# Block-sorted attention with a gated layer on one core: the whole program written as one list, with the picks on ScalarE, the first balancing round alone, six value groups read in place and the first up layer split by units

## The chip, the cores and the metric

One core of one Trainium2 chip runs the kernel. The metric is the device time of one execution in microseconds: 238.96 us for the kernel before, the median of three runs from 238.65 to 239.04.

## The reference

Four batches of eight heads, 768 positions and 64 dimensions. For each head an 8x8 matrix `P` is balanced five times, then keys and values are mixed block by block with it, each query block attends to one mixed block of 96 keys, and the result, heads side by side, goes through a layer with the gate `h * cos(h)`.

```python
for _ in range(5):
    P = P - np.max(P, axis=-1, keepdims=True)
    P = np.exp(P)
    P = P / (np.sum(P, axis=-1, keepdims=True) + 1e-09)
    P = P / (np.sum(P, axis=-2, keepdims=True) + 1e-09)
k_sorted = np.einsum('bhij,bhjcd->bhicd', P, k_b)
v_sorted = np.einsum('bhij,bhjcd->bhicd', P, v_b)
...
scores = scale * np.matmul(q_b, k_sb.transpose(0, 1, 2, 4, 3))
...
h = x @ w_in          # 3072 x 512 by 512 x 2048
g = h * np.cos(h)
return g @ w_out      # 2048 x 512
```

## The kernel before, in words

The 3072 rows are cut into eight chunks `n` of 384 rows; a chunk is half a batch and has four **units** `u` of 96 rows (one query block, all heads). Each chunk goes through scores, softmax, the products with the values (`av`), the turning of their result into `xT`, the up layer (`h`, a cosine on ScalarE, the gate on VectorE) and the down layer (`o`). Later chunks overlap: while chunk `n` is in its up and down layers, the attention of chunk `n+1` is slipped in between.

**The start.** `make_identity` builds `ident` on GpSimd. The loads of queries, keys and values of batch 0 are issued by GpSimd ahead of it, the weights behind. The balancing runs on 32 partitions (L326 to L354): per round one exp on ScalarE (L327) and six instructions on VectorE (L301 to L306). In round 0 the reduction `maskp` (L329), which reads `ident`, stands on VectorE ahead of the round's own six. After round 4 the balanced matrices are in `sorted_by`. `pick` holds zeros and ones: GpSimd clears it (L213) and writes the ones by `affine_select` (L207), three for batches 1, 0, 1 at the start and two for batches 2 and 3 later. A `block` is eight small matmuls of `pick` with `sorted_by` (L360); `spread` (L365) multiplies it with `maskp` into `bd`, the matrix that mixes the blocks. Queries of chunk 0 are turned on TensorE (L315) and copied by ScalarE (L321); `keep_warm` matmuls (L238) on a tile of zeros fill TensorE's waits.

**Keys and values of batch 0.** Three key groups `kp` (L375, 16 matmuls each) and eight value groups `v0` (L662, eight matmuls each) give mixed keys and values; each is copied out of PSUM by ScalarE or VectorE (`k_place`, `v0e`). A value matmul has as its weights the values of one dimension `d` over 96 positions. In `kv`, as loaded, these lie 64 elements apart. GpSimd can copy them into `vperm`, where they lie side by side (L179, 16 dimensions per copy). Before, groups 0 to 3 read `kv` and groups 4 to 7 read `vperm`, after two copies. A matmul writes `w` neighbouring results of 64 columns, of which the first counts and the others are overwritten by the next matmuls: `w` is 3 for groups 0 to 3 and 2 for 4 to 7, less at a group's end.

**Scores to xT, chunk 0.** For each unit: scores on TensorE (L681), maximum and subtraction on VectorE (L698, L702), exp on ScalarE (`p_buf`, L467), transposes on TensorE (L713), their copy `pT` (ScalarE or VectorE), `av` (L514), the division on VectorE (L525, L527), transposes `xps` (L722) and their copy into `xT`. PSUM has three large buffers (`big`) and two small ones (`acc`); a group waits until the copy of its buffer's last owner is done. The four units come in the order 0, 1, 3, 2. The value groups stand between them on TensorE: 3, 1, scores 0, 4, 5, scores 1, 6, 7, scores 3, transposes 0, 2, scores 2, 0.

**First up layer.** `up_four` (L735) makes chunk 0's up layer in halves: two units wide (192 columns), eight matmuls per call; half 0 needs `xT` of units 0 and 1.

The instructions of each engine stand in program order, written out call by call (L782 to L1097), and no engine but TensorE's weight loads departs from it.

Of the kernel before, what the change touches and what calls it, by code (L numbers as in the profile page):

```python
# [14 lines left out]
AX = mybir.AxisListType  # L15


@with_exitstack
def kernel(
# [15 lines left out]
    nc = tc.nc  # L35
# [169 lines left out]
    def picked(t, z, b):  # L205

        nc.gpsimd.affine_select(  # L207
            out=t[:, :, z * PB:(z + 1) * PB], in_=t[:, :, z * PB:(z + 1) * PB],
            compare_op=ALU.not_equal, fill=1.0, base=-b * PB,
            pattern=[[1, nb], [-1, PB]], channel_multiplier=nb)  # L210

    def picks(t, batches):
        nc.gpsimd.memset(t[:], 0.0)  # L213
        for z, b in enumerate(batches):
            picked(t, z, b)
# [7 lines left out]
    picks(pick, (1, 0, 1))  # L223
# [18 lines left out]
    keep_warm(15, big.tile([128, 512], FP32, name="idle", tag="big"))  # L242
# [34 lines left out]
    E, Q = E_eps[:, :, :nb], Q_eps[:, :nb]  # L277
# [21 lines left out]
    def normalize(it, out):  # L299

        nc.vector.reduce_sum(sums[0][:], E_eps[:], axis=AX.X)  # L301
        nc.vector.reciprocal(over[0][:], sums[0][:])
        nc.vector.tensor_tensor(Q, E, by_row(over[0]), op=ALU.mult)
        nc.vector.reduce_sum(sums[1][:], Q_eps.rearrange("p i j -> p j i"), axis=AX.X)
        nc.vector.reciprocal(over[(1, 2, 1, 3, 1)[it]][:], sums[1][:])
        nc.vector.tensor_tensor(out, Q, by_column(over[(1, 2, 1, 3, 1)[it]]), op=ALU.mult)  # L306
# [3 lines left out]
    def q_twice(h2):  # L310
        ps = turns[h2] = acc.tile([128, 2, IC, QR, blk // QR], BF16, name="qps", tag="acc")
        for hp in range(2):
            for r in range(QR):
                for x in range(2):
                    nc.tensor.transpose(  # L315
                        ps[x * D:(x + 1) * D, hp, :, r],
                        q_rows[:, h2 * 2 + hp, r * D:(r + 1) * D], ident[:blk, :blk])

    def q_place(h2):
        dst = q_turned[0][:, :, :QW].rearrange("d e (i h c) -> d h e i c", h=H2, c=blk)  # L320
        A.copy(dst[:, h2], turns.pop(h2).rearrange("d e i r p -> d e i (r p)"))  # L321

    def idle(times):
        keep_warm(times, acc.tile([128, 512], FP32, name="idle", tag="acc"))

    for it in range(5):  # L326
        nc.scalar.activation(E, less[:], AF.Exp)  # L327
        if it == 0:
            nc.vector.reduce_sum(  # L329
                maskp.rearrange("p (b e x) -> p b x e", b=2, e=2),  # L330
                ident.rearrange("p (b x e j) -> p b x e j", b=2, e=2, j=nb), axis=AX.X)
            A.copy(
                order.rearrange("k (p r) -> k p r", r=QR),
                ident[:blk, :blk].rearrange("k (r p) -> k p r", r=QR))
            q_twice(0)
            q_twice(1)
            keep_warm(2, big.tile([128, 512], FP32, name="idle", tag="big"))
        if it >= 2:
            q_place(it - 2)
            if it < 4:  # L340
                idle((6, 2)[it - 2])
                q_twice(it)
            else:
                idle(4)
                q_place(3)
        normalize(it, (less if it < 4 else sorted_by)[:])
        if it == 1:
            nc.gpsimd.tensor_copy(held[:B * H], over[2][:, :1])
            for z in range(3):
                load_w_in(z)  # L350
        if it == 3:
            nc.gpsimd.tensor_copy(held[:B * H], over[3][:, :1])
            load_w_in(3)
            load_q(1)  # L354

    def block(picked, pool=acc, tag="acc"):

        ps = pool.tile([128, nb], FP32, name="bl", tag=tag)
        for j in range(nb):
            nc.tensor.matmul(  # L360
                ps[:], picked[:, j], sorted_by[:, :, j], start=(j == 0), stop=(j == nb - 1))
        return ps

    def spread(dst, ps):
        nc.vector.tensor_tensor(  # L365
            dst[:], maskp.to_broadcast([128, 2 * H, nb]),
            ps[:].unsqueeze(1).to_broadcast([128, 2 * H, nb]), op=ALU.mult)

    blocks = [block(pick[:, :, z * PB:(z + 2) * PB]) for z in range(2)]
    spread(bds[0], blocks[0])  # L370

    MH = H2 * IC

    def k_products(ps, t, c, rows, rhs, keys=kbuf):
        nc.tensor.matmul(  # L375
            ps[:, t], keys[rows, c * 2 * D:(c + 1) * 2 * D], rhs, start=True, stop=True)

    def k_sort_g(t0, eng, pool, tag):
        ps = pool.tile([128, 4, 4 * NB], FP32, name="ks", tag=tag)
        for t in range(4):  # L380
            k_products(ps, t, t0 + t, slice(0, 128), bds[1].rearrange("p x i -> p (x i)"),
                       pair)
        copy_on(
            eng, kT2[:, ::2, :, :, t0:t0 + 4].rearrange("p e b m t -> p b e m t"),
            ps.rearrange("p t (b e m) -> p b e m t", b=2, e=2))

    def k_swap(keys):
# [3 lines left out]
    def hold_keys():  # L391

        nc.gpsimd.tensor_copy(held[:], kT[1][:, 1, 0, :1])
# [14 lines left out]
    def v_cols(d, permuted):  # L408
        return vperm[:, d * blk:d * blk + 128] if permuted else vv[:, d]

    def v_sort_b(b, d0, nd, eng, pool, tag):
        ps = pool.tile([128, nd, 2 * NB], FP32, name="vs", tag=tag)
        rows, xs = slice(0, 64 + b * 64), slice(b * H, (b + 1) * H)
        for t in range(nd):
            nc.tensor.matmul(
                ps[:, t], v_cols(d0 + t, b == 1 or d0 + t >= D // 2)[rows],
                bdv[rows, xs].rearrange("p x i -> p (x i)"), start=True, stop=True)
        copy_on(
            eng, vS[0][:, b * 2 * NB:(b + 1) * 2 * NB, d0:d0 + nd],
            ps[:blk].rearrange("p t n -> p n t"))  # L420

    def v_sort_g(d0, nd, eng, pool, tag):
        ps = pool.tile([128, nd, 4 * NB], FP32, name="vs", tag=tag)
        for t in range(nd):
            nc.tensor.matmul(  # L425
                ps[:, t], v_cols(d0 + t, True), bds[1].rearrange("p x i -> p (x i)"),
                start=True, stop=True)
        copy_on(eng, vS[1][:, :, d0:d0 + nd], ps[:blk].rearrange("p t n -> p n t"))

    def v_at(g, b2, hp, h2, i):  # L430
        return (b2 * 2 + hp) * NB + h2 * nb + i


    LATE = 5
    s_t, pb, pT, xn_t = {}, {}, {}, {}
    xT = {}
    cnt = [0]

    def qk_part(n, u, part, pool, tag):
        w = len(part)  # L440
        sc = pool.tile([128, w, 512], FP32, name="sc", tag=tag)
        for h2 in range(H2):
            for e, hp in enumerate(part):
                scores(sc[:, e, h2 * 128:h2 * 128 + blk], n, u, h2, hp)
        scv = sc[:blk].rearrange("p e (h c) -> p (e h) c", c=128)[:, :, :blk]
        mx = small.tile([blk, w * H2], FP32, name="mx", tag="mx")
        nc.vector.reduce_max(mx[:], scv, axis=AX.X)  # L447
        s = s_t[n, u][:, part[0]:part[0] + w].rearrange("p e h c -> p (e h) c")
        nc.vector.tensor_tensor(s, scv, mx.to_broadcast(list(s.shape)), op=ALU.subtract)  # L449

    def qk(n, u):

        s_t[n, u] = sp.tile([blk, 2, H2, blk], FP32, name="s", tag="s")
        qk_part(n, u, [0, 1], big, "big")

    def qk_half(n, u, hp, pool=None, tag="acc"):

        if hp == 0:
            s_t[n, u] = sp.tile([blk, 2, H2, blk], FP32, name="s", tag="s")
        qk_part(n, u, [hp], pool or acc, tag)  # L460

    def expo(n, u, on_pe=False):
        p = p_bufs[cnt[0] % NP]
        cnt[0] += 1


        nc.scalar.activation(  # L467
            p[:, :, :blk], s_t.pop((n, u)).rearrange("p e h c -> p (e h) c"), AF.Exp,
            scale=scale)
        if n < LATE:  # L470
# [6 lines left out]
        if on_pe:  # L477
            pb[n, u] = p
        else:
            nc.sync.dma_start_transpose(out=t[:], in_=p.rearrange("p a c -> p (a c)"))  # L480

    def hold(t):

        nc.gpsimd.tensor_copy(held[:blk], t[:blk, 0, :1])

    def p_hold(n, u):
        hold(pT[n, u])

    def p_transpose(n, u, eng, pool, tag):
        p = pb.pop((n, u))  # L490
        ps = pool.tile([128, 2 * H2, 128], BF16, name="pps", tag=tag)
        for a in range(2 * H2):
            nc.tensor.transpose(ps[:blk, a, :blk], p[:, a, :blk], ident[:blk, :blk])
# [646 lines left out]
```

## Time and profile before

| | |
|---|---|
| time, median of 3 | 238.96 us (238.65 to 239.04) |
| span of the profiled execution | 236.9 us |
| time minus span | 2.1 us (launch and end, outside the span; the profiled execution's own time is not listed apart from its span) |
| TensorE busy | 228.3 us (96%) |
| VectorE, ScalarE, GpSimd busy | 171.1, 154.0, 93.4 us |
| first matmul of chunk 0's up layer | 29.97 us |
| first matmul of chunk 0's down layer | 41.86 us |

Busy times of engines overlap. A busy TensorE may still be slow, since a matmul that waits for its weights counts as busy; so the time from the start of one matmul to the start of the next is what has to be read. Times in the timeline count from the span's start. A row such as `x8` merges eight neighbouring instructions, its second number is from the first one's start to the last one's end. "PEld" is the weight load of a matmul.

### The profile page before, as it was taken

Reading aid. Unit: us, or ns where it says so; the run is one execution under the profiler, and the core shown is the slowest. Engines: PE = TensorE matmul, PEld = TensorE weight load, DVE = VectorE, ACT = ScalarE, POOL = GpSimd, SP = SyncE. Lnnn points to the kernel's source line nnn. Section 1 sums busy time; section 2 is a strip of 40 time slices with the busy share of each in tenths; the row PEclk is TensorE's granted clock in tenths of the full one; section 3 lists DMA queues with packets and bytes.
Section 4 is the critical chain, followed back from the end, with each engine's and each line's share of the span. In section 5 each row is a group of like instructions: output and inputs, shape, how many; then the busy total and the mean of one; then the engine's idle time right before and its main releaser. Section 6 shows DMA issues by size and latency. Waiting matters only on the chain.

```text
span 236.9 us, 5429 instructions
## 1 busy us (share of the span) xinstructions
PE 228.3 (96%) x2230; PEld 144.0 (61%) x2230; DVE 171.1 (72%) x284; ACT 154.0 (65%) x205; POOL 93.4 (39%) x117
## 2 busy tenths in 40 slices
PE   8699999999999999999999999999999999999994
PEld 2368799567665656655666556655564565555553
DVE  5658976887789666893689976998698769535700
ACT  3356975588889747795688747673767376646611
POOL 7699994894970098940808000800000000000000
PEclk9999999999999999999999999999999999999999
DMA  7999999995899989869899938944972460341012
GB/s 97 203 199 205 203 224 211 148 201 167 102 117 183 146 155 136 160 150 184 95 104 101 116 64 150 209 68 91 119 216 46 80 192 3 55 133 47 0 44 89
DMA packets 66423, 30.89 MB, mean 130 GB/s; under 512 B 55136, under 2 KB 61920, under 8 KB 66144
## 3 DMA queue, kind: packets, MB, share of 16 engines
q0 software_dynamic: 24048, 13.64, 42.1%
q1 hardware_dynamic: 42064, 16.73, 33.4%
q8 instruction: 17, 0.28, 0.5%
q10 hardware_dynamic: 288, 0.20, 0.3%
q14 instruction: 6, 0.05, 0.1%
HBM read 27.27 MB, written 6.29 MB: 142 GB/s over the span
## 4 chain that ended last, share of the span: by engine, by line
PE 81%; DMA 6%; ACT 4%; DVE 4%; issue 3%; POOL 1%; SPq 0%; ACTq 0%; POOLq 0%
PE h L558 31%; PE o L583 21%; DMA pT<-p_buf 5%; PE h L735 5%; PE o L756 4%; PE sc L405 3%; PE av L514 3%; PE ks L375 2%; PE vs L662 2%; ACT p_buf L467 2%; PE o L1104 1%; PE vs L425 1%; PE pps L713 1%; DMA xT<-xn 1%; PE vs L238 1%
## 5 line engine op out<-in xcount | busy, mean ns | idle before, releaser
L558 PE MATMUL h<-xT,w_in_t 128*128 128x384 bf16 x448 | 78.4, 326 | 0.2 <-DMA xT<-xn 0.2
L583 PE MATMUL o<-w_out_t,gg 128*128 128x512 bf16 x320 | 76.5, 379 | 0.0
L566 DVE TENSOR_TENSOR gg<-c,h 128x768 bf16<-128x768 f32 x56 | 52.6, 949 | 18.8 <-ACT c L562 18.8
L562 ACT ACTIVATE c<-h,half_pi 128x768 f32<-128x768 f32 x56 | 50.4, 900 | 22.5 <-PE h L558 21.6
L558 PEld LDWEIGHTS <-w_in_t 128*128 128x128 bf16 x448 | 42.2, 98 | 26.5 <-issue 0.6
L583 PEld LDWEIGHTS <-gg 128*128 128x128 bf16 x320 | 29.1, 98 | 27.6
L467 ACT ACTIVATE p_buf<-s 96x768 bf16<-96x768 f32 x32 | 26.0, 840 | 4.4 <-DVE s L702 2.4
L179 POOL COPY vperm<-kv 64x1536 bf16<-64x1536 bf16 (+1 forms) x10 | 28.0, 2831 | 0.6 <-DMA kv<-in_v_dram 0.6
L449 DVE TENSOR_TENSOR s<-sc,mx 96x384 f32<-96x384 f32 (+1 forms) x33 | 24.3, 735 | 1.8
L447 DVE TENSOR_REDUCE mx<-sc 96x4 f32<-96x384 f32 (+1 forms) x33 | 24.0, 729 | 0.7 <-PE sc L405 0.7
L527 DVE TENSOR_TENSOR xn<-av,r 96x512 bf16<-96x512 f32 x32 | 22.0, 687 | 1.1
L525 DVE RECIPROCAL r<-av 96x8 f32<-96x8 f32 x32 | 6.4, 199 | 14.6 <-PE av L514 14.4
L129 POOL DMA_DIRECT2D kv<-in_q_dram x24 | 15.9, 674 | 0.7 <-issue 0.5
L405 PE MATMUL sc<-kTs,q_turned 128*128 128x96 bf16 x224 | 15.3, 206 | 0.1
L249 ACT COPY kv<-o 128x512 f32<-128x512 f32 (+2 forms) x10 | 5.3, 530 | 14.9 <-PE o L583 12.4
L405 PEld LDWEIGHTS <-q_turned 128*128 128x128 bf16 x224 | 12.6, 98 | 4.0 <-DVE s L449 0.4
L249 ACT CAST kTs<-ks 128x512 bf16<-128x512 f32 (+1 forms) x18 | 11.0, 632 | 5.7 <-PE ks L375 5.7
L756 PE MATMUL o<-w_out_t,gg 128*128 128x512 bf16 x48 | 11.4, 379 | 0.0
L251 DVE COPY kv<-o 128x512 f32<-128x512 f32 (+1 forms) x5 | 3.0, 602 | 11.4 <-PE o L1104 8.5
L129 POOL DMA_DIRECT2D q_mem<-in_q_dram x16 | 10.7, 684 | 1.2 <-DMA kv<-in_v_dram 1.0
L238 PE MATMUL idle<-warm 128*128 128x512 bf16 x29 | 8.5, 436 | 2.8 <-ACT q_turned L321 1.8
L735 PE MATMUL h<-xT,w_in_t 128*128 128x192 bf16 x128 | 11.1, 246 | 0.0
(119 smaller groups left out, 285.0 us busy)
## 6 DMA issues: line engine op xcount, KB each, us to landing
out_dram<-kv SPq DMA_DIRECT2D x12, 256.0 KB, 2.5
out_dram<-o_s SPq DMA_DIRECT2D x10, 256.0 KB, 2.7
w_in_t<-in_moe_w_in_dram POOLq DMA_DIRECT2D x4, 512.0 KB, 11.8
w_out_t<-in_moe_w_out_dram POOLq DMA_DIRECT2D x4, 512.0 KB, 12.6
kv<-in_k_dram POOLq DMA_DIRECT2D x2, 768.0 KB, 10.3
kv<-in_v_dram POOLq DMA_DIRECT2D x2, 768.0 KB, 13.1
pair<-in_k_dram POOLq DMA_DIRECT2D x2, 768.0 KB, 11.0
kv<-in_v_dram POOLq DMA_DIRECT2D x6, 256.0 KB, 5.4
```

The costliest lines, as they stand in the source:

```text
L129: nc.gpsimd.dma_start(out=q_heads[:, i, :, e], in_=src[:, ih * IC + i, :, e])
L179: nc.gpsimd.tensor_copy(dst, src)
L405: nc.tensor.matmul(out, q_of(n, hp)[:, x:x + 128], keys_of(n, u, h2, hp), start=True, stop=True)
L447: nc.vector.reduce_max(mx[:], scv, axis=AX.X)
L449: nc.vector.tensor_tensor(s, scv, mx.to_broadcast(list(s.shape)), op=ALU.subtract)
L467: nc.scalar.activation(p[:, :, :blk], s_t.pop((n, u)).rearrange("p e h c -> p (e h) c"), AF.Exp, scale=scale)
L527: nc.vector.tensor_tensor(xn.rearrange("p h e d -> p e h d"), avv[:, :, :, :D], r.to_broadcast([blk, 2, H2, D]), op=ALU.mult)
L558: nc.tensor.matmul(h[:, f2, :w], w_in_t[:, kk, f * 128:(f + 1) * 128], xT[n][:, kk], start=(kk == 0), stop=(kk == KC - 1))
L562: nc.scalar.activation(c[:], h[:, :, :w], AF.Sin, bias=half_pi[:, 0:1])
L566: nc.vector.tensor_tensor(gt[n, fp // 2][:, f:f + 2], c[:], h[:, :, :w], op=ALU.mult)
L583: nc.tensor.matmul(o[:], gt[n, f // 4][:, f % 4, ts * 128:(ts + 1) * 128], w_out_t[:, f, :], start=(f == 0), stop=(f == FC - 1))
L735: nc.tensor.matmul(o[:, part, f2 * w:(f2 + 1) * w], w_in_t[:, kk, f * 128:(f + 1) * 128], xT[0][:, kk, h * w:(h + 1) * w], start=(kk == 0) ...
```

## The change

All of L308 to L1097 becomes one text, `PLAN`, one call per line, which a loop reads; helpers are renamed and split so that each line issues work on one engine (`S` scores, `M` maximum, `X` subtraction, `E` exp, `TP`/`TE` transposes and their copy, `AV`/`N` products and division, `XP`/`XE` the turning into `xT`, `U`/`C`/`G` up, cosine, gate, `D`/`O`/`W` down, copy and store). What differs in the work:

- `maskp` and `order` (the other early copy) stand behind round 0 on VectorE and behind round 1's exp on ScalarE. First warm-up matmuls: 12 for 15, then 2, 6 and 4 for 2, 6, 2 and 4.
- The five `affine_select` are gone. `pick` is laid out with rows one element longer, so that its ones have a regular step, and ScalarE copies them from `ident`, three in the balancing, two between the last exp of chunk 0 and the copies `pT`.
- Value groups 0 to 5 read `kv` in place, only 6 and 7 read `vperm` (one copy of GpSimd, not two); every value matmul writes 64 columns, none of them overwritten. Order on TensorE: 0, 1, scores 0, 2, 3, 4, scores 1, 5, scores 2, transposes 0, 6, scores 3, 7. Units come in the order 0, 1, 2, 3. The fill matmuls ahead of the groups are seven as before.
- The first half of the first up layer runs by units: `U1` has 32 matmuls of 96 columns on `xT` of one unit, its cosine is one instruction, its gate two. Half 1 stays as it was.
- On GpSimd the values of batch 1 are loaded ahead of its keys, and the queries of chunk 2 behind the four `vperm` copies of batch 1.

From the first matmul of the down layer on, TensorE, VectorE, ScalarE and the store queue have the same instructions in the same order as before, but for the places named.

```diff
-    def picked(t, z, b):
-        nc.gpsimd.affine_select(
-            out=t[:, :, z * PB:(z + 1) * PB], in_=t[:, :, z * PB:(z + 1) * PB],
-            compare_op=ALU.not_equal, fill=1.0, base=-b * PB,
-            pattern=[[1, nb], [-1, PB]], channel_multiplier=nb)
+    def picked(first, n, z, b, eng):
+        w = n * PB + 1
+        d = pair[:B * H, first * PB * nb:first * PB * nb + nb * w].rearrange(
+            "p (j c) -> p j c", c=w)[:, :, z * PB:(z + 1) * PB].rearrange(
+            "p j (h i) -> p h j i", i=nb)[:, :, :, 0]
+        copy_on(eng, d, ident[:B * H, b * H:(b + 1) * H].unsqueeze(2).to_broadcast([B * H, H, nb]))
...
-    for it in range(5):
-        nc.scalar.activation(E, less[:], AF.Exp)
-        if it == 0:
-            nc.vector.reduce_sum(
-                maskp.rearrange("p (b e x) -> p b x e", b=2, e=2),
...
+    VZ, v_wide = 6, 1
...
-            w = min(8 - t, 2 if z > 3 else 3)
+            w = min(8 - t, v_wide)
             nc.tensor.matmul(
-                o[:, t:t + w].rearrange("p w n -> p (w n)"), v_cols(z * 8 + t, z > 3)[:64],
+                o[:, t:t + w].rearrange("p w n -> p (w n)"), v_cols(z * 8 + t, z >= VZ)[:64],
...
+    def U1(u, g):
+        o = kept_tile(("h1", u, g), big, "big", [128, 2, 512], FP32, "h")
+        for z in range(8):
+            f = g * 8 + z
+            for kk in range(KC):
+                nc.tensor.matmul(
+                    o[:, z // 4, z % 4 * blk:(z % 4 + 1) * blk],
+                    w_in_t[:, kk, f * 128:(f + 1) * 128],
+                    xT[0][:, kk, u * blk:(u + 1) * blk], start=(kk == 0), stop=(kk == KC - 1))
+    def G1(u, g, b):
+        if (0, g * 2 + b) not in gt:
+            gt[0, g * 2 + b] = gp.tile([128, 4, TC], BF16, name="gg", tag="gg")
+        nc.vector.tensor_tensor(
+            gt[0, g * 2 + b][:, :, u * blk:(u + 1) * blk],
+            ps["c1", u, g][:, b].rearrange("p (f c) -> p f c", f=4),
+            ps["h1", u, g][:, b, :TC].rearrange("p (f c) -> p f c", f=4), op=ALU.mult)
...
+    for line in PLAN.split("\n"):
+        name, *args = line.split()
```

On VectorE, the start of the first balancing round, before (`P` is the loaded matrix, `less` the input of the exp, `E` its output):

```order
L296 TENSOR_REDUCE top<-P 32x8
L297 TENSOR_TENSOR less<-P,top 32x64
L329 TENSOR_REDUCE maskp<-ident 128x2x4x2
L301 TENSOR_REDUCE sums_150<-E 32x8
L302 RECIPROCAL over_152<-sums_150 32x8
L303 TENSOR_TENSOR Q<-E,over_152 32x64
```

and now:

```order
L1147 TENSOR_TENSOR less<-P,top 32x64
L1151 TENSOR_REDUCE sums_137<-E 32x8
L1152 RECIPROCAL over_139<-sums_137 32x8
L1153 TENSOR_TENSOR Q<-E,over_139 32x64
L1154 TENSOR_REDUCE sums_138<-Q 32x8
L1155 RECIPROCAL over_140<-sums_138 32x8
L1156 TENSOR_TENSOR less<-Q,over_140 32x64
L1196 TENSOR_REDUCE maskp<-ident 128x2x4x2
```

`maskp`, and with it the wait for `ident`, moved from ahead of the round to behind it.

On ScalarE, from the copies of the value groups (`vS`) to the first cosine (`c`), before (`p_buf` is an exp of chunk 0, `pT` and `xT` are copies of transposes):

```order
L249 CAST vS<-vs 96x64x8 x3
L467 ACTIVATE p_buf_106<-s 96x8x96
L249 CAST vS<-vs 96x64x8 x2
L467 ACTIVATE p_buf_107<-s 96x8x96
L249 CAST vS<-vs 96x64x8
L249 COPY pT<-pps 96x768
L249 CAST vS<-vs 96x64x8
L467 ACTIVATE p_buf_108<-s 96x8x96
L467 ACTIVATE p_buf_106<-s 96x8x96
L249 COPY pT<-pps 96x768 x2
L249 COPY xT<-xps 128x4x96
L741 ACT_TABLE_LOAD
```

and now:

```order
L1388 ACTIVATE p_buf_106<-s 96x8x96
L1099 CAST vS<-vs 96x64x8
L1388 ACTIVATE p_buf_107<-s 96x8x96
L1099 CAST vS<-vs 96x64x8 x2
L1099 COPY pT<-pps 96x768
L1099 CAST vS<-vs 96x64x8
L1388 ACTIVATE p_buf_108<-s 96x8x96
L1388 ACTIVATE p_buf_106<-s 96x8x96
L1099 COPY pair<-ident 32x8x8 x2
L1099 COPY pT<-pps 96x768 x2
L1099 COPY xT<-xps 128x4x96
L1544 ACT_TABLE_LOAD
```

The second exp stands one value copy earlier, and two pick copies (`pair<-ident`) stand between the last exp and the last two `pT`.

On GpSimd, around the copies of batch 1's values into `vperm`, before:

```order
L119 DMA q_mem<-in_q_dram 96x8x256
L92 DMA pair<-in_k_dram 128x3072 x2
L179 COPY vperm<-kv 64x1536 x4
L137 MEMSET kv 96x16x64 x2
L129 DMA kv<-in_q_dram 96x4x64 x8
```

and now:

```order
L947 DMA pair<-in_k_dram 128x3072 x2
L1034 COPY vperm<-kv 64x1536 x4
L974 DMA q_mem<-in_q_dram 96x8x256
L947 DMA kv<-in_v_dram 128x1024
L992 MEMSET kv 96x16x64 x2
L984 DMA kv<-in_q_dram 96x4x64 x8
```

The load of chunk 2's queries (`q_mem`) moved from ahead of the four copies to behind them, and the first part of the next values with it.

More of the change, by code (lines that the diff above doesn't have):

```diff
@@ L18 @@
+C 7 2
+G 7 2
+W 6 2
+U 7 3
+C 7 3
+G 7 3
+U 7 4
+C 7 4
+G 7 4
+U 7 5
+C 7 5
+G 7 5
+U 7 6
+C 7 6
+G 7 6
+U 7 7
+C 7 7
+G 7 7
+D 7 0 0
+D 7 0 1
+D 7 0 2
+D 7 0 3
+O 7 0 o A
+W 7 0
+D 7 1 0
+D 7 1 1
+D 7 1 2
+D 7 1 3
+O 7 1 o A
+W 7 1"""
 @with_exitstack
@@ L422, in v_sort_g @@
[L422 to L435, printed above, removed]
@@ L1088 @@
[L1088 to L1097 removed]
+        else:
+            o_s = op.tile([128, Dm], FP32, name="o_s", tag="o_s")
```

1707 lines of the change are left out of this document (1100 added, 607 removed).

## The prediction

> **What bounds the kernel now.** I read the page first, then the chain of waits, then the timeline of the stretch that the change touches.
>
> ```profile
> span 236.9 us, 5429 instructions
> PE 228.3 (96%) x2230; PEld 144.0 (61%) x2230; DVE 171.1 (72%) x284; ACT 154.0 (65%) x205; POOL 93.4 (39%) x117
> PE 81%; DMA 6%; ACT 4%; DVE 4%; issue 3%; POOL 1%; SPq 0%; ACTq 0%; POOLq 0%
> ```
>
> TensorE is the bound: 96% busy and 81% of the chain. From the first down layer on, the order on TensorE is unchanged, so the question is when that layer starts (41.86, row below). Whatever moves it moves the end by as much, unless a later load is then late. All sums are differences against this one execution, whose span is 236.9 us; I add them to the median of the three runs, 238.96. A measurement of this kernel can tell a change from none at about 0.2%, here 0.5 us.
>
> **The start.** The timeline of the balancing, its engines mixed:
>
> ```profile
> 2.80 0.26 ACT L327 ACTIVATE E<-less 32x64 f32<-32x64 f32 x1 [0.56 <-DVE less L297]
> 3.88 0.29 DVE L329 TENSOR_REDUCE maskp<-ident 128x16 f32<-128x128 bf16 x1 [1.11 <-POOL ident masks.py:199]
> 4.09 0.20 DVE L301 TENSOR_REDUCE sums<-E 32x8 f32<-32x72 f32 x1
> 5.24 1.87 POOL L207 TENSOR_SCALAR_AFFINE_SELECT pair<-pair 32x512 bf16<-32x512 bf16 x3
> 5.33 0.63 DVE L306 TENSOR_TENSOR less<-Q,over 32x64 f32<-32x64 f32 x1
> 6.34 0.22 DVE L301 TENSOR_REDUCE sums<-E 32x8 f32<-32x72 f32 x1 [0.39 <-ACT E L327]
> 8.33 0.22 DVE L301 TENSOR_REDUCE sums<-E 32x8 f32<-32x72 f32 x1 [0.38 <-ACT E L327]
> 10.18 0.22 DVE L301 TENSOR_REDUCE sums<-E 32x8 f32<-32x72 f32 x1 [0.38 <-ACT E L327]
> 13.68 0.58 PE L360 MATMUL bl<-sorted_by,pair 32*128 32x8 bf16 x16
> 13.91 5.50 POOL L179 COPY vperm<-kv 64x1536 bf16<-64x1536 bf16 x2 [0.39 <-DMA kv<-in_v_dram]
> ```
>
> `E` of round 0 is ready at 2.80 + 0.26 = 3.06, yet its sums start at 4.09, because `maskp` ahead of them waits for `ident`. With `maskp` behind, the sums start about 3.09: 1.00 gained. A round takes 10.18 - 8.33 = 1.85. Round 0 took 6.34 - 4.09 = 2.25, stretched beside GpSimd's `affine_select` (one `less` alone 0.63), and round 1 8.33 - 6.34 = 1.99. With the three `affine_select` gone both fall to 1.85: 0.54 more. The last piece of `ident` is still being written by GpSimd while round 0's `Q` runs; it can stretch that by up to the 0.14 that round 1 lost, and I take 0.08. The `block` matmuls move from 13.68 to about 12.22, **-1.46** (-1.40 to -1.54). Two things could hide this. The values land at 13.91 (the copy's releaser); their first use is after three key groups, at 16.76 - 1.46 = 15.30 (rows below). The three pick copies on ScalarE stand between exps, each of which is followed by more than 1.2 us of VectorE work; nearest row an exp of the same 32x64, 0.26; so nothing for those.
>
> **The value groups.** TensorE and its weight loads from the keys to scores 1:
>
> ```profile
> 14.51 0.52 PEld L375 LDWEIGHTS <-kv 64*128 64x128 bf16 x16 [0.23 <-issue]
> 16.44 0.39 PE L238 MATMUL vs<-warm 128*128 128x512 bf16 x1
> 16.76 0.80 PEld L662 LDWEIGHTS <-kv 64*128 64x128 bf16 x8 [0.23 <-issue]
> 17.60 0.39 PE L238 MATMUL vs<-warm 128*128 128x512 bf16 x1
> 19.31 0.59 PE L662 MATMUL vs<-bdv,vperm 64*128 64x128 bf16 x8
> 19.84 0.39 PE L238 MATMUL vs<-warm 128*128 128x512 bf16 x1
> 20.57 0.40 PE L681 MATMUL sc<-kTs,q_turned 64*128 64x64 bf16 x14
> ```
>
> A fill occupies 16.76 - 16.44 = 0.32 from start to start, a group in place 17.60 - 16.76 = 0.84, a group from `vperm` 19.84 - 19.31 = 0.53. Ahead of the end of scores 1 (20.57 + 0.40 = 20.97) stood two groups in place and two from `vperm`; now five in place. That adds one fill and one group, 1.16, and 2 x 0.31 where two groups change kind: **+1.78**, provided that a group in place still costs 0.84 when each matmul writes 64 columns in place of 192. No row shows that. What speaks for it are the loads, first the first two of a group, then all of each kind the first two of a group, then all of each kind (least/median/most ns)::
>
> ```profile
> 16.76 0.26 PEld L662 LDWEIGHTS <-kv 64*128 64x128 bf16 x2 [0.23 <-issue]
> L662 PEld LDWEIGHTS <-kv x32: 161/174/227, 16.8 to 25.2; 64*128 64x128 bf16 x32
> L662 PEld LDWEIGHTS <-vperm x32: 92/94/96, 19.3 to 22.0; 64*128 64x128 bf16 x32
> ```
>
> A load with elements 64 apart takes 174 ns, with neighbours 94. The first one alone takes at least 0.16, and the second ends 0.10 later. Eight in a group take 0.80, that is (0.80 - 0.16)/7 = 0.091 each, about the 0.10 of a pair that no long matmul could hold back. So the loads set the pace, not the columns. The bound below is the rate of the keys, which lie together, (0.52 - 0.095)/15 = 0.028 per load: 0.16 + 7 x 0.028 and the 0.04 to the next fill, 0.40 a group. Above, nothing in the rows would make it dearer than 0.84. I take 0.84, since the row of this very load is nearer than that of another layout.
>
> [...]
>
> Scores 1 then end at 20.97 - 1.46 + 1.78 = 21.29, **+0.32**.
>
> **From scores to the up layer.** VectorE, ScalarE and TensorE behind scores 1:
>
> ```profile
> 20.09 0.95 DVE L702 TENSOR_TENSOR s<-sc,mx 96x768 f32<-96x768 f32 x1
> 21.02 0.95 DVE L698 TENSOR_REDUCE mx<-sc 96x8 f32<-96x768 f32 x1
> 25.79 0.95 DVE L702 TENSOR_TENSOR s<-sc,mx 96x768 f32<-96x768 f32 x1
> 27.53 1.62 ACT L249 COPY pT<-pps 96x768 bf16<-96x768 bf16 x2
> 29.05 0.48 ACT L249 COPY xT<-xps 128x384 bf16<-128x384 bf16 x1
> 29.97 2.80 PE L735 MATMUL h<-xT,w_in_t 128*128 128x192 bf16 x32
> 41.86 1.90 PE L756 MATMUL o<-w_out_t,gg 128*128 128x512 bf16 x8
> 43.60 1.18 PE L405 MATMUL sc<-kTs,q_turned 128*128 128x96 bf16 x24
> ```
>
> From the maximum of unit 1 (21.02) VectorE goes with next to no gap through six instructions of 0.95 to 26.74, and the last exp can start. These six are there after too, so the last exp starts 0.32 later. Behind it on ScalarE now stand two pick copies, then the same two `pT` and the `xT` of unit 0. Nothing covers those copies: the two `pT` and the `xT` queue behind them, and TensorE's products and its first up layer wait for these. Nearest row: the exp of 32x64, 0.26; below, a reduction of that size on VectorE takes 0.20. I take 0.23 each: 0.46. `xT` of unit 0, ended 29.05 + 0.48 = 29.53, ends at 29.53 + 0.32 + 0.46 = 30.31. But `U1` needs only this `xT`, where before the two-unit half started at 29.97, 0.44 after it, since it also needed that of unit 1. So the up layer starts at about 30.33: **+0.36** (+0.2 to +0.6).
>
> In it 64 matmuls of 192 columns become 128 of 96. Both rows fit one rate with one tail at the end: 32 x 192 columns in 2.80 and 24 x 96 in 1.18 give 1.62/3840 = 0.42 ns a column and a tail of 0.21. By that the halves are equally long. With the tails spread over all matmuls, two of 96 columns take 2 x 1.18/24 = 0.098 for 2.80/32 = 0.088, 64 x 0.010 = 0.7 more. I take nothing, because a tail belongs to the last matmul alone. The gates on VectorE become two of half the size, the cosine stays one instruction per tile; both lie beside about 2.7 us of TensorE per tile. So the down layer starts at 41.86 + 0.36, and the end is later by as much: 238.96 + 0.36 = **239.3**.
>
> **Loads that move.** On GpSimd, and TensorE's first use of the queries of chunk 2:
>
> ```profile
> 44.38 11.21 POOL L179 COPY vperm<-kv 64x1536 bf16<-64x1536 bf16 x4 [0.20 <-DMA kv<-in_v_dram]
> 47.21 0.40 PE L375 MATMUL ks<-bd,kv 128*128 128x64 bf16 x8
> 58.77 0.90 PE L260 MATMUL qps<-ident,q_mem 96*64 96x96 bf16 x32
> kv<-in_k_dram POOLq DMA_DIRECT2D x1, 768.0 KB, 12.7
> kv<-in_v_dram POOLq DMA_DIRECT2D x1, 768.0 KB, 15.1
> q_mem<-in_q_dram POOLq DMA_DIRECT2D x1, 384.0 KB, 4.9
> ```
>
> Values of batch 1 land at 44.38, the keys ahead of them in the queue 15.1 - 12.7 = 2.4 earlier, or up to 3 with the later issue; now they swap places, and the four copies run from about 41.6 to 52.8. Behind them the query load takes 4.9: 57.7, against its use at 58.77 + 0.36 = 59.1. Cover 1.4; with 15.1 for the values even in front, the load is 1 late. The keys of batch 1 then land at 44.4, ahead of their first use at 47.21 + 0.36; beyond 3 us of delay they would cost what they are late.
>
> **The rivals.**
>
> *B, groups in place run at the rate of neighbouring weights.* 0.40 for 0.84: five groups before scores 1 gain 5 x 0.44 = 2.2. Scores 1 end at 19.1; VectorE is free of unit 0's subtraction (ends 21.04 before, earlier by 1.46 and by two groups' 0.88, so 18.7). The down layer starts 1.85 earlier than before, but the queries of chunk 2 land at 57.7 against 56.9, so 0.8 of it is given back: **237.9** (237.2 to 238.3). For it: nothing but that 192 columns are in the row of 0.80 too. Against it: 0.10 in the pair of loads. Chance 0.14.
>
> *C, slower: the clock of TensorE falls.*
>
> ```profile
> 5.00:10.00 5.00, 3.16 (x43) 1.59 (x42) 3.62 (x15) 1.30 (x4) 4.27 (x8) 1.00 1.16 227
> 7.17 0.61 PE L238 MATMUL idle<-warm 128*128 128x512 bf16 x2
> 9.03 1.47 PE L238 MATMUL idle<-warm 128*128 128x512 bf16 x6 [1.26 <-ACT q_turned L321]
> ```
>
> A fill streams for (1.47 - 0.39)/5 = 0.216. Values now stream 0.216 + 8 x 0.028 = 0.44 of each 1.16 us, 38%, for 5 us. The emptiest stretch of before with a granted clock of 1.00 (third number from the end of the first row) has eight fills from 7.17 to 10.5, 52%. Whether the clock holds at 38% no row shows. It decides from the point where the gate counts such a stretch as idle; at half clock the six fills ahead of scores 1 cost 0.21 more each, 1.3: **240.6** (240.0 to 241.5). Chance 0.12. [...]
>
> *D, slower: the queries of chunk 2 are late*, if batch 1's values take 15.1 even in front: 1.0 beyond the forecast, **240.3**. Chance 0.08.
>
> **How the numbers follow.** Forecast A 0.66: 239.3, own range 238.4 to 240.1 from the unknown picks (0.4 to 0.6), the up layer and the start; of it 0.06 falls below 238.5, 0.36 within 0.5 of before, 0.24 above 239.4. With B 0.14 faster, C 0.12 and D 0.08 slower: faster 0.20, same 0.36, slower 0.44. The range 237.4 to 240.6 leaves out the lower part of B and the upper half of C, together 0.12.
>
> **What would show it.** Block matmuls near 12.2; a group in place 0.84 from its first load to the next fill (0.40 under B); scores 1 ending near 21.3; two `pair` copies of 0.2 to 0.26 behind the last exp; first up matmul near 30.3, the down layer near 42.2; granted clock 1.00 from 12 to 24; no wait of `qps` near 59. The forecast is wrong above all if the loads were held by the 192 columns.

## The result and the profile after

The changed kernel takes 241.53 us, median of four runs from 241.27 to 242.55, beside 238.81 for the kernel before on the same chip: a ratio of 1.011, 95% interval 1.0077 to 1.0143. The forecast was 239.3 with a range to 240.6. The ratios leave out executions over 1.5% above the fastest of their kernel; for four kernels below (`w2`, `before_w1`, `w1_fill4`, `w3_loads`) those are executions in which TensorE's clock had fallen, so clocks are counted over all executions, and for `w2` and `before_w1` nothing rests on the ratio.

The page of the changed kernel:

```profile
span 240.8 us, 5546 instructions
PE 231.6 (96%) x2289; PEld 146.7 (61%) x2289; DVE 171.6 (71%) x288; ACT 156.0 (65%) x210; POOL 89.1 (37%) x111
PEclk9995599999999999999999999999999999999999
```

TensorE is as busy as before. What is new stands in the third line: in the fourth and fifth of 40 slices the granted clock, the share of full speed at which TensorE may run, is half. By windows of that stretch (window, length, busy time of PE, PEld, DVE, ACT and POOL, granted clock, DMA share, GB/s):

```profile
14.00:16.00 2.00, 2.00 (x39) 1.50 (x39) 1.39 (x2) 1.35 (x2) 1.82 (x1) 1.00 1.26 213
16.00:18.00 2.00, 2.00 (x32) 1.66 (x31) 0.81 (x2) 0.69 (x2) 2.00 (x3) 0.75 1.23 203
18.00:20.00 2.00, 2.00 (x13) 1.06 (x12) 1.87 (x2) 0.79 (x2) 2.00 (x4) 0.50 1.24 206
24.00:26.00 2.00, 1.65 (x33) 1.51 (x32) 1.97 (x3) 1.33 (x3) 2.00 (x3) 0.50 1.39 198
30.00:34.00 4.00, 4.00 (x92) 3.77 (x90) 3.09 (x8) 3.42 (x6) 3.93 (x3) 0.92 1.25 209
34.00:38.00 4.00, 4.00 (x99) 4.00 (x96) 2.80 (x8) 2.43 (x4) 2.05 (x6) 1.00 1.20 227
```

A mean of 0.75 over 16 to 18 us says that the clock fell at 17.0, and 0.92 over 30 to 34 that it rose at 30.6: 13.6 us at half speed, over all but the first one and a half value groups and into the products of chunk 0, 2.1 us before the up layer starts. PE counts as busy all through the 3 us ahead of the fall, and in the low stretch too but for about 0.4 us near 26 (1.65 of 2.00, in the row from 24). A share of busy time does not show that little is streamed.

The timeline of the same places as in the prediction, engines mixed:

```profile
2.97 0.26 ACT L1190 ACTIVATE E<-less 32x64 f32<-32x64 f32 x1 [0.73 <-DVE less L1147]
3.26 0.21 DVE L1151 TENSOR_REDUCE sums<-E 32x8 f32<-32x72 f32 x1 [0.32 <-ACT E L1190]
5.11 0.22 DVE L1151 TENSOR_REDUCE sums<-E 32x8 f32<-32x72 f32 x1 [0.19 <-ACT E L1190]
12.30 0.37 PE L1180 MATMUL bl<-sorted_by,pair 32*128 32x8 bf16 x8
15.58 0.90 PE L1292 MATMUL vs<-bdv,kv 64*128 64x64 bf16 x8
16.41 0.39 PE L1088 MATMUL vs<-warm 128*128 128x512 bf16 x1
17.98 0.61 PE L1088 MATMUL vs<-warm 128*128 128x512 bf16 x1
18.52 0.92 PE L1292 MATMUL vs<-bdv,kv 64*128 64x64 bf16 x8
19.37 0.61 PE L1088 MATMUL vs<-warm 128*128 128x512 bf16 x1
21.98 0.67 PE L1352 MATMUL sc<-kTs,q_turned 64*128 64x64 bf16 x14
22.69 0.95 DVE L1370 TENSOR_REDUCE mx<-sc 96x8 f32<-96x768 f32 x1 [2.66 <-PE sc L1352]
29.59 0.74 ACT L1099 COPY pair<-ident 32x64 bf16<-32x64 bf16 x2
31.97 0.48 ACT L1099 COPY xT<-xps 128x384 bf16<-128x384 bf16 x1
32.74 4.25 PE L1537 MATMUL h<-xT,w_in_t 128*128 128x96 bf16 x96
44.82 1.90 PE L1559 MATMUL o<-w_out_t,gg 128*128 128x512 bf16 x8
61.60 0.90 PE L1110 MATMUL qps<-ident,q_mem 96*64 96x96 bf16 x32
67.72 0.33 PE L1339 MATMUL sc<-kTs,q_turned 128*128 128x96 bf16 x4 [1.81 <-DMA kTs<-kTs]
```

The start gained nearly what was worked out: a first round of 5.11 - 3.26 = 1.85, block matmuls at 12.30, 1.38 earlier than before. A value group in place takes 16.41 - 15.58 = 0.83 at full clock with 64 columns. At half clock it takes 19.37 - 18.52 = 0.85, but the fill ahead of it 18.52 - 17.98 = 0.54 in place of 0.32. Scores 1 end at 22.65, the up layer starts at 32.74 and the down layer at 44.82, 2.96 later than before. TensorE does not wait for the queries of chunk 2 (61.60); later on a wait of scores for `kTs` is new. This profile is of the slowest of the four executions (242.55): from the start of the down layer to the end of the span it takes 240.8 - 44.82 = 196.0, about 1 us more than the kernel before (195.0). The second profile of this kernel (`after_again`, 241.33) has its down layer at 44.86 and takes 194.7 from there.

### The profile page after: what moved, and what is told of

Same layout as the page of the kernel before. It is cut to its first block, busy times and chain, and to the rows that moved or that the text cites. A ratio compares the mean times of both kernels' runs of the same rounds, so it can differ in the third digit from the quotient of the medians.

```text
span 240.8 us, 5546 instructions
## 1 busy us (share of the span) xinstructions
PE 231.6 (96%) x2289; PEld 146.7 (61%) x2289; DVE 171.6 (71%) x288; ACT 156.0 (65%) x210; POOL 89.1 (37%) x111
## 4 chain that ended last, share of the span: by engine, by line
PE 80%; DVE 7%; DMA 6%; ACT 4%; issue 1%; SPq 0%; ACTq 0%
PE h L1490 28%; PE o L1559 27%; PE sc L1339 3%; PE av L1430 3%; DMA vperm<-p_buf 3%; PE h L1537 2%; PE h L1513 2%; PE vs L1292 2%; DMA kTs<-kTs 2%; PE ks L1234 2%; PE vs L1316 2%; PE o L1641 1%; PE pps L1412 1%; PE vs L1088 1%; PE xps L1464 1%; DVE mx L1370 1%
## 5 line engine op out<-in xcount | busy, mean ns | idle before, releaser
L1490 PEld LDWEIGHTS <-w_in_t 128*128 128x128 bf16 x448 | 42.3, 98 | 26.1
L1559 PEld LDWEIGHTS <-gg 128*128 128x128 bf16 x368 | 33.3, 98 | 31.9
L1370 DVE TENSOR_REDUCE mx<-sc 96x8 f32<-96x768 f32 (+1 forms) x41 | 31.6, 772 | 5.5 <-PE sc L1352 3.5
L1034 POOL COPY vperm<-kv 64x1536 bf16<-64x1536 bf16 (+1 forms) x9 | 25.3, 2857 | 2.5 <-DMA kv<-in_v_dram 2.5
L1099 ACT COPY xT<-xps 128x384 bf16<-128x384 bf16 (+1 forms) x10 | 5.1, 511 | 9.7 <-PE xps L1464 9.6
L1099 ACT CAST vS<-vs 96x512 bf16<-96x512 f32 x15 | 8.5, 583 | 3.9 <-PE vs L1292 3.8
## 6 DMA issues: line engine op xcount, KB each, us to landing
w_in_t<-in_moe_w_in_dram POOLq DMA_DIRECT2D x4, 512.0 KB, 13.6
kv<-in_k_dram POOLq DMA_DIRECT2D x2, 768.0 KB, 12.5
```

Of the source, the lines that this page charges most:

```text
L1034: nc.gpsimd.tensor_copy(dst, src)
L1099: eng.copy(dst, src)
L1370: nc.vector.reduce_max(mx[:], s_view(n, u, hp), axis=AX.XY if n < 2 else AX.X)
L1490: nc.tensor.matmul(o[:, f2, :TC], w_in_t[:, kk, f * 128:(f + 1) * 128], xT[n][:, kk], start=(kk == 0), stop=(kk == KC - 1))
L1559: nc.tensor.matmul(out_ps[n, ts][:], gt[n, q][:, f % 4, ts * 128:(ts + 1) * 128], w_out_t[:, f, :], start=(f == 0), stop=(f == FC - 1))
```

## The experiments

All run beside the kernel before. Theory G says that TensorE's clock falls because too few columns are streamed in the value stage; what grants the clock is called the gate below. Its rivals: S, the new start or the number of groups in place brings the clock down; L, the groups in place are bound by their columns; K, the moved loads cost time through `kTs`.

### w3: the width put back

```diff
-            w = min(8 - t, v_wide)
+            w = min(8 - t, 2 if z >= VZ else 3)
```

> The changed kernel with the width of the value matmuls put back: 192 columns in place, 128 from vperm, all else as changed. Theory G (the clock of TensorE halves because too few columns stream in the value stage): granted clock 1.00 from 12 to 30 us, a group in place still about 0.84 from its first load to the next fill, scores 1 ending near 21.4, the down layer near 42.3, 0.7 to 1.5% less time than the changed kernel; within 0.5 us of the kernel before if the wait for kTs near 66 us goes too, 1 to 2 us above it if that wait stays. Rival S (the clock falls because of the new start or the number of groups in place): clock 0.50 again from about 17 us, time 241.0 to 242.0. Rival L (the groups in place are held by their columns): with the clock at 1.00 a group takes longer than the 0.83 seen with 64 columns.

239.94 us (ratio to before 1.0041, 1.0021 to 1.0061). The granted clock is 0.997 or more in 12 of 12 executions, and was 0.979 or less in all four of the changed kernel. (A mean a little under 1.00 need not be a fall in the work: in the kernel before, 0.998, the clock falls at 235.9 us, behind the last matmul.) Its timeline, and one window:

```profile
12.31 0.37 PE L1180 MATMUL bl<-sorted_by,pair 32*128 32x8 bf16 x8
15.59 0.92 PE L1292 MATMUL vs<-bdv,kv 64*128 64x192 bf16 x8
16.45 0.39 PE L1088 MATMUL vs<-warm 128*128 128x512 bf16 x1
21.21 0.44 PE L1352 MATMUL sc<-kTs,q_turned 64*128 64x64 bf16 x14
21.69 0.95 DVE L1370 TENSOR_REDUCE mx<-sc 96x8 f32<-96x768 f32 x1 [1.79 <-PE sc L1352]
28.20 0.75 ACT L1099 COPY pair<-ident 32x64 bf16<-32x64 bf16 x2
30.18 0.46 ACT L1099 COPY xT<-xps 128x384 bf16<-128x384 bf16 x1
30.69 4.37 PE L1537 MATMUL h<-xT,w_in_t 128*128 128x96 bf16 x96
42.88 1.90 PE L1559 MATMUL o<-w_out_t,gg 128*128 128x512 bf16 x7
64.67 0.33 PE L1339 MATMUL sc<-kTs,q_turned 128*128 128x96 bf16 x4 [0.71 <-DMA kTs<-kTs]
```

```profile
18.00:20.00 2.00, 2.00 (x17) 1.57 (x17) 1.86 (x2) 0.92 (x2) 2.00 (x5) 1.00 1.24 206
```

Nothing but the width differs from the changed kernel, and the columns that it adds are overwritten at once. Three times the columns cost 0.03 per group (16.45 - 15.59 = 0.86 for 0.83) and keep the clock at 1.00. The down layer starts 1.94 earlier than in the changed kernel. L falls: a group does take longer than 0.83, but by 0.03 for three times the columns. S falls as far as the start and the groups in place are not enough by themselves. The other 1.02 us of the down layer's delay against the kernel before is not the clock's.

### w2 and before_w1: between, and the width alone

`w2` has `w = min(8 - t, 2)` in the changed kernel; `before_w1` is the kernel before with one line changed:

```diff
-            w = min(8 - t, 2 if z > 3 else 3)
+            w = 1
```

> The changed kernel with 128 columns in every value matmul. Streaming per group and fill rises from 0.44 to about 0.62 of 1.16 us (53%). Theory G: if the point lies between 38% and 52%, clock 1.00 and the time of the run with 192 columns; if it lies above 53%, clock 0.50 from about 17 us and the time of the changed kernel. Rival S: clock 0.50 and 241.0 to 242.0 whatever the width.

> The kernel before with 64 columns in every value matmul and nothing else changed. Theory G: the clock falls here too, after the second or third value group (near 19 us), and stays 0.50 until the up layer streams (near 30 us): 1.5 to 3.5 us slower than before. Rival S (start, number of groups in place): clock 1.00 and a time within 0.5 us of before. The groups from vperm stream 52% of their time, so a fall that ends early (half of the cost) is possible under G.

`w2`: the clock was under 0.98 in 6 of 10 executions, 0.992 to 1.00 in the others; times from 239.36 to 244.41. `before_w1`: under 0.98 in 5 of 12, 0.991 to 1.00 in seven; times from 238.19 to 245.80. The kernel before itself, over the 96 executions that these studies shared, was never under 0.99. In the profiled execution of `before_w1` the clock falls in this window:

```profile
18.00:20.00 2.00, 2.00 (x35) 1.42 (x34) 1.30 (x2) 0.83 (x2) 2.00 (x2) 0.94 1.22 201
```

A mean of 0.94 puts the fall at 19.8, near the 19 that G expected; by the windows behind it the clock rises at 36.9. So the width alone can bring the clock down without the new start, and S falls as something that is needed for it; and where the clock holds, the narrow groups cost nothing (238.19 to 239.96 with a clock of 0.99 or more). It is not all or nothing: with two of four groups ahead of scores 1 in place it falls in under half of the executions, in the changed kernel, with five of five, in all. These two kernels differ in the start too, so what makes a fall more frequent is not separated. In `w2` G had expected one outcome for all executions; it was in between, and in the profiled one the clock fell at 22.1, not near 17.

### w1_fill4 and w3_nofill: streaming without wide value matmuls, and without fills

`w1_fill4` keeps 64 columns and has four fills ahead of each of five groups (`v0 0 c 1` becomes `v0 0 c 4`, and so on); `w3_nofill` has 192 columns and none (`v0 0 c`).

> The changed kernel, 64 columns per value matmul kept, but four fill matmuls ahead of each of the first five value groups in place of one. Streaming is then 4 x 0.216 + 8 x 0.028 = 1.09 of about 1.81 us, 60%, in place of 38%. Theory G (the share of streamed columns decides): granted clock above 0.99 in most executions although the matmuls are as narrow as in the changed kernel; the fills cost 5 x 3 x 0.216 = 3.2 us on the way to scores 1, so the down layer starts near 46 and the time is 1.5 to 3.5 us above the run with 192 columns. Rival W (the narrow value matmuls themselves bring the clock down): clock 0.96 to 0.98 as in the changed kernel, time 243 to 245.

> 192 columns in place, and no fill matmuls ahead of the value groups. Streaming is 21 x 64 columns, 0.56 of 0.84 us, 67%, the same share as with the fills. Theory G: clock as in the run with fills (above 0.99 in nearly all executions), scores 1 end 5 x 0.32 = 1.6 us earlier, near 20.0, the up layer up to 1.6 earlier unless copies of the value groups hold the buffers; time 0.5 to 1.6 us under the run with fills. Rival (the gate needs the long fills): clock 0.96 to 0.98 and a time of 240 to 242.

`w1_fill4` took 244.51 us (1.0187, 1.0115 to 1.0258), clocks from 0.976 to 0.993. In its windows the clock holds through all of the filled groups, to 27.6, and falls only behind them:

```profile
22.00:24.00 2.00, 2.00 (x16) 1.29 (x16) 0.00 (x0) 1.10 (x2) 1.79 (x6) 1.00 1.30 208
26.00:28.00 2.00, 1.15 (x33) 0.96 (x32) 1.97 (x3) 1.09 (x2) 1.89 (x5) 0.91 1.26 207
34.00:38.00 4.00, 4.00 (x97) 3.79 (x94) 2.98 (x7) 3.14 (x4) 2.23 (x6) 0.94 1.24 235
```

So narrow matmuls as such do not bring it down, and W is out by these windows. The numbers that G had forecast were missed: a clock above 0.99 in at least two of four executions, and a time 1.5 to 3.5 us above `w3`, where 4.6 was measured, inside W's range. `w3_nofill` was a miss for G as I had put it: 239.80 us (1.0034, 1.0002 to 1.0066), the same as with fills, and a clock of 0.971 to 0.986 in ten of ten:

```profile
20.00:22.00 2.00, 1.81 (x50) 1.48 (x47) 1.97 (x3) 0.91 (x2) 1.90 (x4) 1.00 1.23 205
22.00:24.00 2.00, 1.25 (x18) 0.97 (x17) 1.97 (x3) 2.00 (x5) 1.83 (x5) 0.95 1.29 204
34.00:38.00 4.00, 4.00 (x94) 4.00 (x93) 2.32 (x6) 2.18 (x3) 1.98 (x6) 0.99 1.23 234
```

In this execution the clock held through the groups in place (1.00 in the row from 20), as G expected from their share of 67%, but fell at 23.8 in the emptier stretch behind them (1.25 of 2.00 us busy), and what the missing fills had gained was given back: scores 1 end at 18.92 + 0.44 = 19.36 for 21.65 in `w3`, but the down layer starts at 44.12 for 42.88. The rival that the fills are needed is out for the value stage only. How much streaming over what time the gate wants is left open; these runs only bracket it.

### after_again: the changed kernel once more

> The changed kernel once more, unchanged, beside the other three on one chip, to see in how many executions the clock falls. Theory G: mean granted clock 0.96 to 0.98 in nearly all of them, median 241.0 to 242.0. Rival (the first four executions were unlucky): half of the executions with a clock above 0.99 and a median under 240.5.

242.70 us, ratio 1.0139 (1.0083 to 1.0194), granted clock 0.963 to 0.970 in four of four. With the first runs that makes eight of eight: it was no bad luck. The median lies above the 241.0 to 242.0 that was expected.

### w3_loads: the loads put back

`Lq 2` stands ahead of the two `Lpk` again and `Lpv 2 6` behind `Lpv 1 6`, width as in `w3`.

> 192 columns as in the first run, and the queries of chunk 2 and the part of the next values are issued where they stood before (queries ahead of the four vperm copies, three parts together). Theory K (the 1.81 us wait for kTs near 66 us comes from these loads colliding with the kTs swap): no wait of sc for kTs, time 0.5 to 1.8 us less than the first run. Rival (that wait belongs to one execution, or to the later start): same time as the first run within 0.3 us.

239.83 us (1.0017, 0.9994 to 1.0040) beside 239.94 for `w3`, intervals that overlap: nothing to be told apart. K predicted that the wait of scores near 65 us goes; in this execution 0.84 us of it stands at the same place, put down to a cosine. `s01_picks_loads` shows it again with the loads in their old place. K falls. Why that wait exists in every profiled kernel with the new list, and in none with the old one, stays open.

The wide columns do not make the clock safe. One of these twelve executions (243.45) has a mean clock of 0.979, and the profiled one falls behind the value groups, from 26.1 to 29.5:

```profile
26.00:28.00 2.00, 2.00 (x25) 1.87 (x23) 1.89 (x4) 1.98 (x4) 1.95 (x4) 0.52 1.26 207
```

### w3_s01: scores 1 ahead of the value groups

```diff
 v0 2 B 1
+S 0 1 B
 M 0 0
 v0 3 c 1
...
 v0 4 c 1
-S 0 1 B
...
+S 0 2 B
 v0 5 B
-S 0 2 B
```

> 192 columns, and on TensorE scores 1 stand ahead of value group 3 (behind 4 before) and scores 2 ahead of group 5 (behind it before). Theory D (the chain from scores 1 over six VectorE instructions and the last exp sets the start of the up layer): the maximum of unit 1 starts near 19.9, right behind the subtraction of unit 0, 1.8 us earlier; the last exp 1.8 earlier; the up layer 0.8 to 1.8 us earlier than 30.69, unless the last value groups are late in place of it. Rival V (the value groups on TensorE set it): the up layer starts within 0.3 us of 30.69.

238.49 us, ratio 0.9975 (0.9951 to 1.0000), clock 0.991 or more in ten of ten. Its timeline:

```profile
12.53 0.37 PE L1180 MATMUL bl<-sorted_by,pair 32*128 32x8 bf16 x8
20.03 0.94 DVE L1370 TENSOR_REDUCE mx<-sc 96x8 f32<-96x768 f32 x1
29.17 0.46 ACT L1099 COPY xT<-xps 128x384 bf16<-128x384 bf16 x1
29.69 4.24 PE L1537 MATMUL h<-xT,w_in_t 128*128 128x96 bf16 x96
41.76 1.90 PE L1559 MATMUL o<-w_out_t,gg 128*128 128x512 bf16 x7
```

The maximum of unit 1 (20.03 for 21.69) now follows VectorE's own work, 1.66 earlier, and the up layer comes 1.00 earlier, 1.22 counted from the block matmuls. So scores 1 lie on the path to the up layer, and the value groups ahead of them cost the changed kernel time beside the clock; V as it was put is out. But only part of the 1.66 arrives, and not the 1.8 that D expected for the last exp: the exp of unit 2, one ahead of the last, from which the chain of waits runs on to the up layer, starts at 25.73 for 26.68. In this run the chain that leads to that exp goes over the value groups on TensorE and ScalarE's copies of them, so behind scores 1 they are the next bound, as V had it.

### s01_picks, s01_picks_vz4 and s01_picks_loads: towards a better version

To `w3_s01`: `b_pick 3 A` and `b_pick 4 A` move behind `XE 0 0 A`; then `VZ, v_wide = 4, 1` and `vp 32` ahead of `vp 48`, or the loads as in `w3_loads`.

> The run with scores 1 ahead of group 3, and the two late pick copies moved on ScalarE from behind the last exp to behind the copy xT of unit 0. Theory (the picks lie on the path, 0.37 each by the trace, as 0.74 in a row): xT of unit 0 and the first up matmul 0.4 to 0.7 us earlier than 29.69, time 0.3 to 0.7 us less than the run with scores 1 moved alone. Rival (transposes xps or the products set xT by then): the first up matmul within 0.2 us of 29.69.

> As the run before it, and groups 4 and 5 read vperm again (a second vperm copy on GpSimd). Theory: each of the two costs 0.53 in place of 0.84 from start to start, but both stand behind scores 1 now, so the last value groups come 0.6 us earlier and the up layer gains 0 to 0.6. Rival: the second copy of GpSimd, done near 19.4, makes group 4 wait, or the clock falls in the emptier stretch: no gain or a loss up to 1.5.

> The run with scores 1 moved and the late picks moved, with the loads of chunk 2's queries and of the next values issued where they stood before the change. Theory: a candidate to beat both kernels; median 237.6 to 238.3, 0.3 to 0.7% under the kernel before, clock above 0.99 in nearly all executions; the loads are worth 0 to 0.5 us. Rival: the wait of scores for kTs near 64 us stays whatever the loads' place, so the time is that of the run before it, within 0.3 us.

`s01_picks` took 238.08 us, ratio 0.9952 (0.9928 to 0.9975). In the profiled execution TensorE waited 1.60 us for the first queries, 0.89 in `w3_s01`, and its clock was at half long ahead of the value groups, by the fills from about 9.1 on (two from 8.45 take 0.61, three from 9.24 take 1.44), up to 12.5 (0.88 over 12 to 14); so I count from the block matmuls:

```profile
14.53 0.37 PE L1180 MATMUL bl<-sorted_by,pair 32*128 32x8 bf16 x8
30.72 0.48 ACT L1099 COPY xT<-xps 128x384 bf16<-128x384 bf16 x1
31.24 0.42 PE L1430 MATMUL av<-vS,pT 96*128 96x65 bf16 x8
31.49 4.25 PE L1537 MATMUL h<-xT,w_in_t 128*128 128x96 bf16 x96
```

`xT` of unit 0 ends 30.72 + 0.48 - 14.53 = 16.67 after them, 0.43 sooner than the 29.17 + 0.46 - 12.53 = 17.10 of `w3_s01`: the price of the picks on the path. The up layer gains only 0.20 (16.96 for 17.16), because TensorE's products (`av`) ahead of it are last. `s01_picks_vz4` gained nothing, 238.94 us (0.9990, 0.9955 to 1.0024; one of its twelve executions took 394.74, at a mean clock of 0.556, cause unknown): a value group waited 0.9 us for GpSimd's copies into `vperm`, as its rival said.

`s01_picks_loads` took 238.20 us, ratio 0.9959 (0.9941 to 0.9977), not told apart from `s01_picks`:

```profile
63.44 0.33 PE L1339 MATMUL sc<-kTs,q_turned 128*128 128x96 bf16 x4 [1.15 <-DMA kTs<-kTs]
```

### before_start: the new start alone

The kernel before, with `maskp` and the early copy emitted behind round 0, and the first three picks as ScalarE copies behind the exps of rounds 1 and 2:

```diff
-    picks(pick, (1, 0, 1))
+    nc.gpsimd.memset(pick[:], 0.0)
...
-        if it == 0:
+        if it == 1:
             nc.vector.reduce_sum(
                 maskp.rearrange("p (b e x) -> p b x e", b=2, e=2),
...
+            picked_on(1, 0)
+            picked_on(2, 1)
+        if it == 2:
+            picked_on(0, 1)
```

> The kernel before with the new start alone: maskp and the early copy behind round 0, the first three picks copied by ScalarE, no affine_select in the balancing; value groups, order and up layer as before. Theory P (the prediction's sum of the start, 1.46, is right and was eaten by the value groups): block matmuls near 12.3 in place of 13.68, the up layer near 28.6 and the down layer near 40.5 in place of 41.86, time 1.0 to 1.6 us under the kernel before, clock above 0.99. Rival H (the gain is hidden, since the loads of keys and values or the vperm copies set the value groups): the down layer within 0.4 us of 41.86 and no change in time.

238.32 us, ratio 0.9959 (0.9932 to 0.9987): about 1 us of the forecast 1.46 arrives at the end. In the profiled execution:

```profile
12.71 0.58 PE L372 MATMUL bl<-sorted_by,pair 32*128 32x8 bf16 x16
14.79 5.57 POOL L179 COPY vperm<-kv 64x1536 bf16<-64x1536 bf16 x2 [1.89 <-DMA kv<-in_v_dram]
20.42 0.20 PE L674 MATMUL vs<-bdv,vperm 64*128 64x64 bf16 x1 [0.67 <-POOL vperm L179]
20.89 0.95 DVE L710 TENSOR_REDUCE mx<-sc 96x8 f32<-96x768 f32 x1 [0.81 <-PE sc L693]
41.72 1.90 PE L768 MATMUL o<-w_out_t,gg 128*128 128x512 bf16 x7
```

The block matmuls start 13.68 - 12.71 = 0.97 earlier here, where P expected 12.3. The values landed at 14.79, and group 5 on TensorE waited for GpSimd's copies until 20.42, so the maximum of unit 1 started at 20.89, 0.13 earlier than before, and the down layer 0.14 earlier. This execution took 239.23, as much as the median of the kernel before; one that shows the gain was not profiled. So in this execution H's wait takes the gain, while the median gains about 1 us: both P and H hold in part, and how much of the start's sum the wait takes in the faster executions is not shown. Reading `kv` in place, as the change does, avoids that wait and pays for it with dearer groups.

## Why the prediction was wrong

- **The start** was nearly right: block matmuls forecast at 12.22, seen at 12.30, a gain of 1.38 where the range was 1.40 to 1.54. The first round took 1.85; the sums of that round began at 3.26, not 3.09.
- **A value group in place** was right: 0.84 forecast, 0.83 seen with 64 columns. Rival B is out. Loads set the pace, since columns do not (0.86 with 192), and not at TensorE's clock, since 0.85 is taken at half of it. So what the prediction named as the main way to be wrong, loads held by the 192 columns, was not it.
- **The step that failed** is the clock. The sum took all fills, scores and products at 1.00, "granted clock 1.00 from 12 to 24". The prediction had worked out that streaming falls to 38% against 52% in the emptiest stretch of before, named the consequence as rival C, and gave it a chance of 0.12. It fell in eight of eight executions. The change cut the columns that were overwritten, as if they only cost time, and these had been what kept the clock up. C's price was 1.3 us for six fills; between `w3` and the changed kernel the down layer moves by 44.82 - 42.88 = 1.94, of which 22.65 - 21.65 = 1.00 stands up to the end of scores 1. The rest comes behind it, where the price had nothing: eight transposes of a unit, for one, take 0.85 for 0.52. So C's own range, to 241.5, was just too low.
- The chance of 0.12 for C was my estimate, and no run stood behind it beyond the stretch at 52%. C lets its price begin where the gate "counts such a stretch as idle"; no run shows what the gate counts. What they show in its place: the clock fell at 17.0 with TensorE busy in 2.00 of 2.00 us ahead of it (the row from 14), and a fill then took 0.22 more (0.54 for 0.32), where C had 0.21. A stretch without gaps that streams little was enough.
- **Terms mis-sized beside the clock.** `w3` has a down layer at 42.88 where 42.22 was forecast. The block matmuls come 0.09 later. From them to the end of scores 1 it took 21.65 - 12.31 = 9.34 in place of 9.07; 0.20 of that stands ahead of the first value group (15.59 - 12.31 = 3.28, before 16.76 - 13.68 = 3.08), which the sum took as unchanged. The up layer to the down layer took 42.88 - 30.69 = 12.19 in place of 11.89: the first 96 matmuls of 96 columns take 4.20 us to the next instruction, 0.0437 each for the 0.040 that the prediction's 0.42 ns a column gives. The 0.7 that it weighed for this and set to nothing was 0.3 here, and 0.2 in the changed kernel (44.82 - 32.74 = 12.08). These misses make 0.66 of the down layer's delay against the forecast, the clock the other 1.94.
- **The picks** delay `xT` of unit 0 by about the 0.46 that was forecast (0.43 by `s01_picks`), but this is in part luck: the two copies take 0.75 in a row, not 2 x 0.23, and the copy behind them starts before they end (28.48, before 28.95, in `w3`). The up layer itself depends less on them, 0.20 by `s01_picks`. From scores 1 to the up layer the forecast 9.04 came out as 30.69 - 21.65 = 9.04; the two terms in it, dearer by the picks and cheaper since `U1` needs one `xT`, are confirmed only together.
- **The chain** from scores 1 to the up layer was right in that scores 1 are on it, as `w3_s01` shows; that all six VectorE instructions set its length is not shown, since an earlier start of them moved the up layer by only 1.00 of 1.66.
- **Loads.** The queries of chunk 2 were in time, so the prediction's rival D is out. The wait for `kTs` (0.7 to 1.8 us) was not foreseen, and its cause is not settled. In `w3` it costs nothing that is seen at the end, 237.1 - 42.88 = 194.2 after its down layer starts, for 195.0 in the kernel before; in the profiled execution of the changed kernel, with the longest wait, it took 196.0.

## What to carry to other kernels

Ahead of removing work from TensorE that seems wasted, add up what is still streamed per microsecond there: a stage whose matmuls are bound by weight loads can lose the clock although the engine counts as busy throughout (here 2.00 of 2.00 us ahead of the fall), and the price is then paid in the stages behind it too (eight transposes 0.85 for 0.52) for as long as the clock stays low, here 6.8 to 17.1 us where the value matmuls were narrow. Put the work that a long serial chain waits for (here scores 1, ahead of the value groups) in front, and check what an earlier start runs into (here a copy that begins when a load lands, at 14.79 in `before_start`). An effect of the clock can show in some executions only (in `w2` in 6 of 10), so look at the granted clock of each and not at one profile.

## What the runs showed of the hardware

- In five profiled executions the low stretches come in whole steps. Worked out of the windows as above, the clock was low for 13.6 us in the changed kernel (17.0 to 30.6), 17.1 in `before_w1` (19.8 to 36.9), 10.3 in `w3_nofill` (23.8 to 34.1), 6.8 in `w1_fill4` (27.6 to 34.5) and 3.4 in `w3_loads` (26.1 to 29.5): 4, 5, 3, 2 and 1 times 3.4 us. Why their lengths are such multiples, and why the clock falls in some executions of `w2` and `before_w1` and not in others, is not shown here.
- A weight load of 128 columns that lie 64 elements apart paces a group at about 0.09 us per load ((0.79 - 0.16)/7 in the changed kernel), the same at full and at half clock of TensorE (0.79 for eight loads from 15.58 and from 18.52, 0.83 and 0.85 for a group), while a fill goes from 0.32 to 0.54.
